# Sharing one feed-forward network between two steps, with 512 tokens side by side in its first layer

## Chip, cores and metric

The kernel runs on one core of one Trainium2 chip. The metric is device time in microseconds (us). Kernels were compared on the same chip in the same rounds; medians and ratios are of fast runs alone.

## The reference

A gated linear recurrence (batch 4, 8 heads, 768 tokens, head dimension 48) is followed by a two-layer network with a PReLU between its layers. All is fp32.

```python
for t in range(S):
    state = f[:, :, t, :, None] * state + einsum('bhd,bhe->bhde', k[:, :, t], v[:, :, t])
    y[:, :, t] = einsum('bhd,bhde->bhe', q[:, :, t], state)
# bridge: (B,H,S,D) -> (B*S, H*D) = (3072, 384)
h = x @ w_in                                        # 384 -> 2048
g = np.maximum(h, 0.0) + alpha * np.minimum(h, 0.0)
out = g @ w_out                                     # 2048 -> 384
```

## The kernel before

There are 12 steps. One step takes two batches and a chunk of 128 tokens, so T = 256 tokens. It prepares decayed keys and queries (`prepare`, VectorE and ScalarE), carries the state on (`carry`), attends (`attend`), and sends its 256 tokens through the network (`network`). The program is written as generators. A string for each step fixes the order in which their pieces are issued, and this order is kept on TensorE (PE), VectorE (DVE) and ScalarE (ACT). P is a piece of this step's preparation, Q one of the next step's, O one of carry (off and pk; then pd and the state), S one of attend (raw and qu for each half; copies into A; py; the result xT), n one of a network.

```python
def network(bp, c, x):
    xT = x["T"]
    gs = []
    for f in range(0, NF, 2):                       # NF = 16 tiles of 128, NK = 3
        ph = bank(...)                              # 128 x 512 in PSUM, 4 banks in turn
        for j in range(2):
            for kt in range(NK):
                nc.tensor.matmul(ph[:, j * T:(j + 1) * T], lhsT=w_in_sb[:, kt, ...],
                                 rhs=xT[:, kt], start=(kt == 0), stop=(kt == NK - 1))
        nc.scalar.activation(neg, phv, AF.Relu, scale=-1.0)
        for j in range(2):
            nc.vector.scalar_tensor_tensor(g[:, j], neg[:, j], om[...], phv[:, j], ALU.mult, ALU.add)
        gs.append(g)
        yield
    po = [bank(...) for u in range(U)]
    for f in range(NF):
        for u in range(U):
            nc.tensor.matmul(po[u][:, 0:DM], lhsT=gs[f // 2][:, f % 2, u * C:(u + 1) * C],
                             rhs=w_out_sb[:, f], start=(f == 0), stop=(f == NF - 1))
        if f % 4 == 3 and f != NF - 1:
            yield
    ...                                             # copies out, DMA
    yield
# cut: four strings for steps 0 to 3
usual = "O n2 S n2 S2 n O n Q n Q n S n2 S Q n S Q2 n Q"
```

A network is thus 12 pieces: 8 of the first layer and 4 of the second. While step n attends, the network of step n-1 fills PE. off, pk, pd, raw, qu and py share two pair buffers in PSUM, so each of them waits until an earlier one has been read out.

## Time and profile before

| | before |
|---|---|
| median time, 4 runs | 659.25 us (658.71 to 660.06) |
| span of the profiled execution | 658.4 us |
| PE busy | 615.5 us, 93% |
| one step from 110 us on | 50.33 us, PE busy throughout |
| one network on PE | 41.4 us |
| PE in attention, one step | 9.0 us |
| VectorE busy, one step | 33.3 us, of it 6.9 for g |

The profile's lines behind these are in the prediction. An fp32 matmul of the program is two records in the trace (1152 first-layer records for 576 products). In a row of the groups, the number after the bar is the busy time, then the mean duration of one, then the idle time ahead of it with what ended it. In a row of the timeline, that idle time stands in brackets with its releaser. The granted clock (PEclk in a page) is the share of TensorE's full clock that the profile shows as granted.

### The profile page before, as it was taken

To read this page: it belongs to the slowest core of one execution; us is meant where nothing else is said; L and a number is where in the kernel's file an instruction comes from. 1 tells how busy PE (TensorE), PEld (TensorE's weight loads), DVE (VectorE), ACT (ScalarE), POOL (GpSimd) and SP (SyncE) were. 2 spreads that over 40 slices of the span, in tenths; PEclk is the share of its full clock that TensorE was granted. 3 is DMA by queue.
4 is the path that set the end of the run, shared out by engine and by line. 5 is a ranking of instruction groups with operands and counts; after the bars stand their busy time and mean duration, and the time that the engine had idled before them with its cause. 6 is when DMAs were issued, how large, how long until landed. Compare 5 with 4: busy or idle time off the path is not lost.

```text
span 658.4 us, 17032 instructions
## 1 busy us (share of the span) xinstructions
PE 615.5 (93%) x7392; PEld 458.0 (70%) x7392; DVE 420.2 (64%) x897; ACT 267.0 (41%) x493; POOL 69.9 (11%) x109
## 2 busy tenths in 40 slices
PE   0548899999999999999999999999999999999997
PEld 0436766866876876876876876876876786786874
DVE  5999889693863685685585586486387486360220
ACT  5855882543443242451451550550460451431210
POOL 8222332000010000000000001001001000000000
PEclk9857999999999999999999999999999999999999
DMA  6979986122212122112013113023023011001000
GB/s 225 302 207 269 282 233 159 35 65 73 66 37 68 35 52 87 33 40 86 28 53 81 31 62 81 26 66 80 26 66 81 26 34 25 26 2 25 24 1 24
DMA packets 29129, 53.03 MB, mean 81 GB/s; under 512 B 4320, under 2 KB 16864, under 8 KB 29056
## 3 DMA queue, kind: packets, MB, share of 16 engines
q0 software_dynamic: 9616, 27.92, 15.4%
q1 hardware_dynamic: 13584, 21.63, 10.6%
q10 hardware_dynamic: 5856, 2.40, 1.7%
q8 instruction: 58, 0.95, 0.6%
q14 instruction: 15, 0.12, 0.1%
HBM read 36.21 MB, written 4.72 MB: 62 GB/s over the span
## 4 chain that ended last, share of the span: by engine, by line
PE 84%; issue 7%; POOL 4%; DVE 2%; ACT 1%; DMA 1%; POOLq 0%
PE po L502 36%; PE ph L486 35%; PE py L456 3%; PE qu L431 3%; PE raw L416 3%; PE pk L369 2%; PE pd L381 2%; POOL w_in_sb L191 1%; PE off L356 1%; POOL w_out_sb L191 1%; DMA w_out_sb<-w_out_lead 1%; DVE us L289 0%; POOL vs L138 0%; ACT A L340 0%; POOL vs L247 0%
## 5 line engine op out<-in xcount | busy, mean ns | idle before, releaser
L486 PE MATMUL ph<-xT,w_in_sb 128*128 128x256 f32 x1152 | 264.3, 387 | 10.3 <-DMA xT<-y 10.3
L502 PE MATMUL po<-w_out_sb,g 128*128 128x384 f32 x768 | 253.0, 488 | 0.3 <-DMA w_out_sb<-w_out_lead 0.3
L486 PEld LDWEIGHTS ph<-xT,w_in_sb 128*128 128x128 f32 x1152 | 218.1, 192 | 44.7 <-DMA w_in_sb<-w_in_lead 11.3
L502 PEld LDWEIGHTS po<-w_out_sb,g 128*128 128x128 f32 x768 | 144.9, 190 | 97.7 <-DMA w_out_sb<-w_out_lead 0.9
L494 DVE SCALAR_TENSOR_TENSOR g<-neg,om,ph 128x256 f32<-128x256 f32 x192 | 83.1, 476 | 152.0 <-ACT neg L491 151.9
L491 ACT ACTIVATE neg<-ph 128x512 f32<-128x512 f32 x96 | 57.7, 601 | 152.8 <-PE ph L486 124.8
L508 ACT COPY o<-po 128x384 f32<-128x384 f32 x24 | 11.5, 478 | 115.2 <-PE po L502 115.2
L436 DVE COPY_PREDICATED ad<-mquad,qu 128x224 f32<-128x224 int32 (+6 forms) x168 | 50.3, 300 | 8.5 <-DVE ad L422 0.5
L465 ACT COPY y<-py 128x512 f32<-128x512 f32 x24 | 12.9, 591 | 81.2 <-PE py L456 81.2
L289 DVE TENSOR_TENSOR us<-us,fs 128x768 f32<-128x768 f32 (+2 forms) x72 | 44.5, 618 | 0.3
L422 DVE COPY_PREDICATED ad<-mraw,raw 128x256 f32<-128x256 int32 (+1 forms) x96 | 42.3, 441 | 2.7
L445 ACT COPY A<-ad 32x256 f32<-32x256 f32 x96 | 38.4, 400 | 3.8 <-DVE ad L436 2.5
L391 DVE TENSOR_TENSOR vs<-vs,f 48x768 f32<-48x768 f32 x20 | 19.1, 953 | 30.4 <-PE py L456 30.0
L275 ACT COPY us<-qd 128x256 f32<-128x256 f32 x48 | 29.6, 666 | 12.2 <-DVE qd L258 7.4
L258 DVE TENSOR_TENSOR qd<-qd,f 128x768 f32<-128x768 f32 (+2 forms) x36 | 27.1, 752 | 8.2 <-ACT qd L253 8.2
L340 ACT COPY A<-q 48x512 f32<-48x512 f32 x48 | 29.6, 617 | 6.3 <-DMA xT<-y 5.5
L237 POOL DMA_DIRECT2D k<-in_kT x11 | 8.4, 761 | 222.6 <-PE raw L416 197.6
L456 PEld LDWEIGHTS py<-A,vs 128*64 128x64 f32 x768 | 25.1, 145 | 7.2 <-issue 6.2
L431 PE MATMUL qu<-us,k 48*32 48x112 f32 x1536 | 26.4, 265 | 2.6 <-DVE us L289 1.7
L456 PE MATMUL py<-A,vs 128*64 128x64 f32 x768 | 26.9, 231 | 0.9 <-DVE vs L397 0.8
L356 PE MATMUL off<-q,kh 48*32 48x32 f32 x768 | 9.4, 199 | 18.3 <-DVE q L307 18.3
L416 PEld LDWEIGHTS raw<-qd,k 48*32 48x32 f32 x1536 | 18.1, 108 | 10.6 <-issue 10.2
(64 smaller groups left out, 451.1 us busy)
## 6 DMA issues: line engine op xcount, KB each, us to landing
w_in_raw<-in_w_in SPq DMA_DIRECT2D x12, 511.8 KB, 5.9
w_out_raw<-in_w_out SPq DMA_DIRECT2D x12, 511.8 KB, 5.8
f<-in_fT POOLq DMA_DIRECT2D x11, 512.0 KB, 4.1
q<-in_qT POOLq DMA_DIRECT2D x11, 512.0 KB, 4.1
k<-in_kT POOLq DMA_DIRECT2D x11, 512.0 KB, 4.3
out<-o SPq DMA_DIRECT2D x24, 192.0 KB, 1.9
vs<-in_v POOLq DMA_DIRECT2D x22, 192.0 KB, 3.5
w_in_sb<-w_in_lead POOLq DMA_DIRECT2D x12, 256.0 KB, 6.1
```

Source lines behind the costliest of these rows:

```text
L275: nc.scalar.copy(q4[:, :, :, r], qdv[r][:, :, :, 0])
L289: nc.vector.tensor_tensor(us[:, :, UO[m]:UO[m] + 4 * n].rearrange("p g (i r) -> p g i r", r=4), us[:, :, skip:skip + 4 * n].rearrange("p g ...
L416: nc.tensor.matmul(raw[DB * j:DB * (j + 1), par, hp * C:hp * C + QW], lhsT=k[r_, g * DB:(g + 1) * DB], rhs=qd[r_, g], start=True, stop=True)
L422: nc.vector.copy_predicated(adu[:, :, :, d:4], mraw[:, d, :, d:4].bitcast(I32).unsqueeze(1).broadcast_to((128, H, NB, n)), rv[:, :, QO[d]: ...
L431: nc.tensor.matmul(qu[DB * j:DB * (j + 1), par, hp * UW + 4:(hp + 1) * UW], lhsT=k4[r_, g * DB:(g + 1) * DB], rhs=us[r_, g, 4:UW], start=T ...
L436: nc.vector.copy_predicated(ad[:, u, :, :, 4 * m:DB], mquad[:, lo:lo + n].bitcast(I32).unsqueeze(1).unsqueeze(1).broadcast_to((128, 2, HP, ...
L445: nc.scalar.copy(A[s_, u, :, s_], ad[s_, u].rearrange("p r h t -> p (r h) t"))
L456: nc.tensor.matmul(py[64 * par:64 * par + 64, u, o:o + CH], lhsT=vs[bp][:, cc, u, hd * D:hd * D + 64], rhs=A[:, u, par * HP + hp, CH * cc: ...
L486: nc.tensor.matmul(ph[:, j * T:(j + 1) * T], lhsT=w_in_sb[:, kt, (f + j) * 128:(f + j + 1) * 128], rhs=xT[:, kt], start=(kt == 0), stop=(k ...
L491: nc.scalar.activation(neg, phv, AF.Relu, scale=-1.0)
L494: nc.vector.scalar_tensor_tensor(g[:, j], neg[:, j], om[:, f + j:f + j + 1], phv[:, j], ALU.mult, ALU.add)
L502: nc.tensor.matmul(po[u][:, 0:DM], lhsT=gs[f // 2][:, f % 2, u * C:(u + 1) * C], rhs=w_out_sb[:, f], start=(f == 0), stop=(f == NF - 1))
```

## The change

The last eight steps (chunks 2 to 5 of both batch pairs) share a network in twos. The first layer then has 512 moving columns for one loaded weight tile instead of 256. The intent: half as many first-layer matmuls and weight loads, and half as many VectorE operations behind them. A pair's network can begin only when both its steps have attended, so the order strings from step 4 on are new. The core of the diff (in code and diffs, `...` stands for what is cut):

```diff
-    def network(bp, c, x):
-        xT = x["T"]
-        for f in range(0, NF, 2):
+    def network(xs):
+        n = len(xs["steps"]) * T
+        per = 512 // n
+        xT = xs["T"]
+        for f in range(0, NF, per):
             ...
-                    nc.tensor.matmul(ph[:, j * T:(j + 1) * T], ..., rhs=xT[:, kt], ...)
+                    nc.tensor.matmul(ph[:, j * n:(j + 1) * n], ..., rhs=xT[:, kt, 0:n], ...)
+            # second half of a pair's g: in the buffers where raw weights came in
-        po = [...]
+        for k, (bp, c) in enumerate(xs["steps"]):
+            po = [...]                              # as before, once for each step of the pair
...
+        "S n2 S Q S n O Q n O S n Q2 n S2 n3 Q",       # step 4:  9 network pieces
+        "P S O S O Q S Q n2 S Q2 S2 n Q2",             # step 5:  3
-    usual = "O n2 S n2 S2 n O n Q n Q n S n2 S Q n S Q2 n Q"
+    usual = (
+        "S n4 O n2 S n S Q n3 O S Q n Q2 n S n2 Q n3 S",   # steps 6, 8, 10:  17
+        "O n S n P S n Q S n Q n O Q S Q n Q S2 Q n",      # steps 7, 9, 11:   7
+    )
```

Networks that are ready queue up, and each `n` takes the next piece of the queue. What remains after the last step is issued at the end, without attention between: 24 pieces instead of 12.

More of the change, by code (lines that the diff above doesn't have):

```diff
@@ L220, in halves @@
         return slice(CH * cc, CH * cc + CH), slice(CH * (1 - cc), CH * (1 - cc) + D)
-    def fill():
-        while True:
-            b = bank("warm")
-            nc.tensor.matmul(b[:, 0:256], lhsT=ones[:, 0:128], rhs=ones[:, 0:256], start=True, stop=True)
-            yield
     def prepare(bp, c, x):
@@ L465, in attend @@
             nc.scalar.copy(y[:, u].rearrange("p h t -> p (h t)"), py[:, u])
-        xT = x["T"] = work.tile([128, NK, T], F32, tag="xT", name=f"xT_{i}")
+        xs = x["xs"]
+        if "T" not in xs:
+            xs["T"] = work.tile([128, NK, B // U * T], F32, tag="xT", name=f"xT_{i}")
+        t0 = xs["steps"].index((bp, c)) * T
+        xT = xs["T"][:, :, t0:t0 + T]
         for hd in range(H):
@@ L476, in attend @@
         yield
-    def network(bp, c, x):
-        i = f"{bp}_{c}"
-        xT = x["T"]
+    def network(xs):
+        i = "{}_{}".format(*xs["steps"][0])
+        n = len(xs["steps"]) * T
+        per = 512 // n
+        xT = xs["T"]
         gs = []
-        for f in range(0, NF, 2):
+        for f in range(0, NF, per):
             ph = bank(f"ph{f}_{i}")
-            for j in range(2):
+            for j in range(per):
                 for kt in range(NK):
-                    nc.tensor.matmul(ph[:, j * T:(j + 1) * T], lhsT=w_in_sb[:, kt, (f + j) * 128:(f + j + 1) * 128],
-                                     rhs=xT[:, kt], start=(kt == 0), stop=(kt == NK - 1))
-            neg = work.tile([128, 2, T], F32, tag="neg", name=f"neg{f}_{i}")
-            phv = ph.rearrange("p (j t) -> p j t", j=2)
-            nc.scalar.activation(neg, phv, AF.Relu, scale=-1.0)
-            g = work.tile([128, 2, T], F32, tag="g", name=f"g{f}_{i}", bufs=8)
-            for j in range(2):
-                nc.vector.scalar_tensor_tensor(g[:, j], neg[:, j], om[:, f + j:f + j + 1], phv[:, j],
-                                               ALU.mult, ALU.add)
-            gs.append(g)
-            yield
-        po = [bank(f"po{u}_{i}") for u in range(U)]
-        for f in range(NF):
-            for u in range(U):
-                nc.tensor.matmul(po[u][:, 0:DM], lhsT=gs[f // 2][:, f % 2, u * C:(u + 1) * C], rhs=w_out_sb[:, f],
-                                 start=(f == 0), stop=(f == NF - 1))
-            if f % 4 == 3 and f != NF - 1:
-                yield
-        for u in range(U):
-            o = work.tile([128, DM], F32, tag="o", name=f"o{u}_{i}")
-            nc.scalar.copy(o, po[u][:, 0:DM])
-            t0 = ((U * bp + u) * NC + c) * C
-            nc.sync.dma_start(out=out[t0:t0 + C], in_=o)
-        yield
@@ new lines, in network @@
+                    nc.tensor.matmul(ph[:, j * n:(j + 1) * n], lhsT=w_in_sb[:, kt, (f + j) * 128:(f + j + 1) * 128],
+                                     rhs=xT[:, kt, 0:n], start=(kt == 0), stop=(kt == NK - 1))
+            neg = work.tile([128, 512], F32, tag="neg", name=f"neg{f}_{i}")
+            nc.scalar.activation(neg, ph, AF.Relu, scale=-1.0)
+            if per == 2 or f < NF // 2:
+                g = work.tile([128, 512], F32, tag="g", name=f"g{f}_{i}", bufs=8)
+            elif f % 2 == 0:
+                both = work.tile([128, 2, 512], F32, tag="raw", name=f"g{f}_{i}", bufs=RAWS)
+                g = both[:, 0]
+            else:
+                g = both[:, 1]
@@ new lines, in network @@
+            for j in range(per):
+                nc.vector.scalar_tensor_tensor(g[:, j * n:(j + 1) * n], neg[:, j * n:(j + 1) * n], om[:, f + j:f + j + 1],
+                                               ph[:, j * n:(j + 1) * n], ALU.mult, ALU.add)
+                gs.append(g[:, j * n:(j + 1) * n])
+            yield
+        for k, (bp, c) in enumerate(xs["steps"]):
+            po = [bank(f"po{u}_{bp}_{c}") for u in range(U)]
+            for f in range(NF):
+                for u in range(U):
+                    t = k * T + u * C
+                    nc.tensor.matmul(po[u][:, 0:DM], lhsT=gs[f][:, t:t + C], rhs=w_out_sb[:, f],
+                                     start=(f == 0), stop=(f == NF - 1))
+                if f % 4 == 3 and f != NF - 1:
+                    yield
+            for u in range(U):
+                o = work.tile([128, DM], F32, tag="o", name=f"o{u}_{bp}_{c}")
+                nc.scalar.copy(o, po[u][:, 0:DM])
+                t0 = ((U * bp + u) * NC + c) * C
+                nc.sync.dma_start(out=out[t0:t0 + C], in_=o)
+            yield
@@ L530, in begin, with networks @@
         if n >= len(steps):
-            return [None] * 4
-        x = {}
-        return [stage(*steps[n], x) for stage in (prepare, carry, attend, network)]
-    with tc.manual_schedule(engines={mybir.EngineType.PE, mybir.EngineType.DVE, mybir.EngineType.Activation}):
-        prep, car, att, net = begin(0)
-        filling = fill()
-        before = None
-        for n in range(len(steps) + 1):
-            coming, carried, following, after = begin(n + 1)
-            on = pieces | {"P": prep, "O": car, "S": att, "z": filling, "n": before, "Q": coming}
-            for key in (first[n] if n < len(first) else usual).split():
+            return [None] * 3
+        x = {"xs": groups[n]}
+        return [stage(*steps[n], x) for stage in (prepare, carry, attend)]
+    groups = []
+    for n, (bp, c) in enumerate(steps):
+        if c < 2 or bp == 0:
+            groups.append({"steps": [(bp, c)]})
+        else:
+            groups[-1]["steps"].append((bp, c))
+            groups.append(groups[-1])
+    ready = []
+    def networks():
+        for xs in ready:
+            yield from network(xs)
+    with tc.manual_schedule(engines={mybir.EngineType.PE, mybir.EngineType.DVE, mybir.EngineType.Activation}):
+        prep, car, att = begin(0)
+        net = networks()
+        for n in range(len(steps)):
+            coming, carried, following = begin(n + 1)
+            on = pieces | {"P": prep, "O": car, "S": att, "n": net, "Q": coming}
+            for key in (first[n] if n < len(first) else usual[n % 2]).split():
                 for _ in range(int(key[1:] or 1)):
@@ L545 @@
                         next(on[key[0]])
-            before, prep, car, att, net = net, coming, carried, following, after
+            if groups[n]["steps"][-1] == steps[n]:
+                ready.append(groups[n])
+            prep, car, att = coming, carried, following
+        for _ in net:
+            pass
 def _level_masks():
```

## The prediction

> **What bounds the kernel now.** I read the page first: its busy shares, its slices and its costliest groups.
>
> ```profile
> PE 615.5 (93%) x7392; PEld 458.0 (70%) x7392; DVE 420.2 (64%) x897; ACT 267.0 (41%) x493; POOL 69.9 (11%) x109
> ...
> PE   0548899999999999999999999999999999999997
> ...
> PEclk9857999999999999999999999999999999999999
> ...
> L486 PE MATMUL ph<-xT,w_in_sb 128*128 128x256 f32 x1152 | 264.3, 387 | 10.3 <-DMA xT<-y 10.3
> L502 PE MATMUL po<-w_out_sb,g 128*128 128x384 f32 x768 | 253.0, 488 | 0.3 <-DMA w_out_sb<-w_out_lead 0.3
> L486 PEld LDWEIGHTS ph<-xT,w_in_sb 128*128 128x128 f32 x1152 | 218.1, 192 | 44.7 <-DMA w_in_sb<-w_in_lead 11.3
> L494 DVE SCALAR_TENSOR_TENSOR g<-neg,om,ph 128x256 f32<-128x256 f32 x192 | 83.1, 476 | 152.0 <-ACT neg L491 151.9
> ```
>
> TensorE is busy 93% of the span, and the slices show that what is missing lies in the first six slices (weights arriving) and in the last. A busy PE may still be pipelined slack, so I went to the chain that ended last, in order of time, for one middle step and for the end:
>
> ```profile
> 313.20 5.18 PE ph L486 x24
> ...
> 331.00 7.97 PE ph L486 x36
> 338.96 10.32 PE po L502 x32
> 349.29 2.02 PE py L456 x64
> ...
> 613.68 20.72 PE ph L486 x96
> 634.40 20.65 PE po L502 x64
> ```
>
> No other engine stands in this stretch of the chain. The last network stands alone: 20.72/96 = 215.8 ns for each first-layer record and 20.65/64 = 322.7 ns for each second-layer one. In the middle of the kernel, 32 second-layer records take 10.32 us, again 322.5 ns each. So the interleaved network streams as fast as the bare one: nothing is hidden in the "busy". One network costs 41.4 us. The windows view, one window for each step of the steady part, shows the rest:
>
> ```profile
> 210.75:261.09 50.34, 50.34 (x619) 37.48 (x618) 33.32 (x70) 17.16 (x33) 3.38 (x5) 1.00 0.20 57
> 261.09:311.42 50.33, 50.33 (x618) 37.47 (x617) 33.34 (x70) 19.42 (x37) 3.38 (x5) 1.00 0.20 56
> ```
>
> The columns are the length, then the busy time of PE, PEld, DVE, ACT and POOL. A step is 50.33 us, PE is busy for all of it, the granted clock is 1.00, DVE works 33.3 us. Attention therefore takes PE 50.3 - 41.4 = 9.0 us a step. From about 103 us to the end PE streams without a gap: **the bound is TensorE's streaming itself**, and the time can fall only by making PE do less or by mending the start.
>
> **What the Trainium skill says.** "TensorE: Matmul & The Clock Gate", section "Wait — 56ns, not 53.3ns?": start to start is N/2.4 ns plus about 2.5 ns fixed per matmul, once warm. "FP8 and Floating Point Precision", section "TensorE Precision Notes": true fp32 takes four passes. The program issues 48 first-layer products a step (16 tiles by 3) and the trace holds 96 records, so a record is two passes: 512/2.4 + 2.5 = 215.8 ns and 768/2.4 + 2.5 = 322.5 ns. The trace agrees to the tenth of a ns. The first page's "LDWEIGHTS" section gives columns/1.2, thus 107 ns for 128; here it is 190 to 192 ns. It differs, but it stays below 215.8 and is hidden. "Perfetto Trace Analysis", section "Optimizing Scalar/DVE Operations", says that each DVE operation has a fixed access overhead, more on PSUM, so larger operations pay it less often. The trace agrees in kind: in the groups with shapes kept apart, at L289 a 128x256 operation takes 423 ns and a 128x512 one 684 ns, 162 ns less than twice as long.
>
> **The change, part by part.**
>
> *Wider first layer.* Eight steps hold 8 x 96 = 768 records of 256 columns. They become 384 records of 512. Columns streamed are the same; what goes is 384 fixed costs: 384 x 2.5 ns = **-1.0 us**. A wide record should be 1024/2.4 + 2.5 = 429.2 ns (estimate from the two widths above). Weight loads are halved for these steps, but they were hidden: no gain.
>
> *ACT and DVE.* ACT evicts the same 512-wide banks at 601 ns, as many as before. DVE replaces two 256-wide operations by one of 512: 476 + (684 - 423) = 737 ns against 952. Each pair of steps has 16 such operations in place of 32; over four pairs 64 x 0.215 = 14 us of DVE duration is saved. DVE has 17 us a step to spare, so this is worth **0 us** on the path where PE is dense.
>
> *Second layer, outputs, memory.* Same 512 records of 384 columns in these steps; the second half of g borrows the buffers in which raw weights came in, free by then. **0 us**.
>
> *Where the network's work lies.* This is the part that can cost. I counted the pieces in the order strings (a first-layer piece is 2.59 us, a second-layer piece 5.16 us, twelve to a step's network). Steps 0 to 3 keep their strings, so the start, with its 43 us of idle PE, stays. Before, every later step held 12 pieces. Now step 4 has 9, step 5 has 3, then even steps have 17 and odd ones 7, and 24 pieces follow the last step. In the even steps PE has 16 x 2.57 + 5.16 + 9.0 = 55 us and DVE 26.4 (33.3 less the 6.9 of g) + 16 x 0.74 = 38; in the odd ones PE has 7 x 5.16 + 9.0 = 45 and DVE 26.4. PE stays the bound there. The bare end of 83 us is dense too: the before's end shows it.
>
> But steps 4 and 5 have one network between them, since a pair cannot start until both its halves are attended. PE work: 2 x 9.0 + 41.4 = **59.4 us**. DVE must do two steps of attention (2 x 26.4, less some 2 that may lag) and g of network 3 (6.9): **58 us**. The two are equal, so each wait that one has for the other shows. Placing them by hand, from trace durations (raw+qu 1.7 us, off and pk 1.7, pd 1.1; DVE's evictions of one raw/qu pair 4.2 us, from the timeline at 226.28 to 230.55): in step 4 the second layer's second bank waits for a late g, and off/pk for a pair buffer, about **2 us**. Step 5 opens with raw, qu, off, pk, raw, qu, pd and no network between them; with two pair buffers, pk waits for DVE's first eviction, raw for ACT, pd for DVE again: about 11 us for 6.2 us of work, **5 us** idle. At the end of step 5 the last second-layer piece runs out while DVE is still making step 6's keys and queries, which qu of step 6 needs: **2 to 3 us**. That is 9 to 10; DVE's busy time by union is a little under the elapsed times I added, so I take **+8 us**.
>
> *Hand-over of xT.* The wide first layer starts after py, one second-layer piece and raw+qu: 5.16 + 1.7 = 6.9 us. In the timeline at 301 us, py ends at 300.9, the last transfer is issued by 306.2 and lands some 2 to 2.8 us later, but the part for the first 128 rows is issued first, some 5.7 us after py. **0 to 1 us** over four hand-overs.
>
> Sum: 659.1 - 1.0 + 8 + 0 to 1 = **666 us**.
>
> **The rivals.** *Dense throughout:* the strings of steps 4 and 5 were plainly placed with care, and if PE finds work in all of them only the 1.0 us (and a few tenths from fewer switches between attention and network) remains: 657 to 658. For it: DVE and PE sums are within 2 us of each other, and DVE's g is cheaper later. Against it: no network is left for step 5 to put between its small matmuls. *Starved harder:* steps 4 and 5 become a pure latency chain over PE, DVE and ACT, ACT's xT issues block its copies (the before's waits show ACT held 5.5 us by them once), and gaps of over 3 us let the clock fall, as in the slices around 20 to 60 us where 7 and 5 tenths were granted beside idle PE. That would add 5 to 8 us more: 671 to 674. *A real gain from fewer weight loads:* if loads, 458 us of PEld, shared the path, halving 768 of them would save tens of us; the spacing of exactly 215.8 ns against a 190 ns load speaks against it. It would give 640 or less. *DVE's relief shortening the path:* only where DVE bounds, that is in step 5, where g is already over; nothing.
>
> **Range and chances.** The floor is some 657 because PE's streaming is fixed; the term that may vary is the idle in steps 4 and 5, 0 to 14 us. I choose 666, with 656 to 672 for 8 in 10. A gain of 2% needs 646, for which no idle time is there to be taken: 0.02. A loss of 2% needs over 672.3, so 13 us of idle: 0.11. Within 2%: 0.87.
>
> **What would show it.** Right: first-layer records of 512 columns spaced at 429 ns, second-layer ones at 322.5; PE gaps of 6 to 10 us in sum between about 215 and 285 us and nearly none after; DVE's g at some 740 ns; an end of 82.5 us with only ph and po. The width's step is wrong if a wide record is not 429 ns. The placement step is wrong if PE has no gaps in steps 4 and 5, or if gaps return at each start of a pair with xT as releaser. The whole is wrong if the time before 210 us moves, since nothing there changes.

## The result, and the profile after

| | before | changed |
|---|---|---|
| median of 4 runs | 659.25 us | 667.37 us (664.29 to 669.22) |
| again, in a later round | 659.66 us (11 runs) | 665.41 us (664.72 to 666.78, 4 runs) |
| ratio, first and later round | | 1.0117 (1.0077 to 1.0158), 1.0090 (1.0075 to 1.0105) |
| PE records | 7392 | 7008 |

A ratio is the mean time of one kernel's fast runs over that of the other's of the same rounds, so it is not quite the ratio of the medians quoted. The change costs about 1%.

The changed kernel's page, busy shares and slices:

```profile
PE 616.2 (93%) x7008; PEld 386.7 (58%) x7008; DVE 412.8 (62%) x833; ACT 265.3 (40%) x493; POOL 68.2 (10%) x109
...
PE   0648899999999988999999999999999999999997
...
PEclk9987999999999997999999999999999999999999
```

71 us of weight loading and 7 us of VectorE time are gone by union (overlapping stretches counted once), and PE is as busy as it was. New are the two eights among the nines of PE (the 15th and 16th slice, 232 to 265 us), with a lower granted clock in the second of them: this is where step 5 opens. The groups with shapes kept apart, and the end of the timeline of PE:

```profile
L487 PE MATMUL ph<-xT,w_in_sb 128*128 128x512 f32 x384 | 168.8, 595 | 0.0
...
L501 DVE SCALAR_TENSOR_TENSOR g<-neg,om,ph 128x512 f32<-128x512 f32 x64 | 47.0, 745 | 74.1 <-ACT neg L491 73.5
```

```profile
576.41 41.36 PE L487 MATMUL ph<-xT,w_in_sb 128*128 128x512 f32 x96
617.61 41.44 PE L511 MATMUL po<-w_out_sb,g 128*128 128x384 f32 x128
```

In the bare end (the last network, with no attention beside it) 96 wide records start at 576.41 and the next kind at 617.61: 429.2 ns each, as worked out. The last pair's network is as dense as a single one. Step 5 in the same timeline, start and duration first:

```profile
248.42 1.08 PE L349 MATMUL off<-q,kh 48*32 48x32 f32 x64 [2.07 <-DVE ad L415]
250.82 1.94 PE L362 MATMUL pk<-ident,ks 128*128 128x128 f32 x8 [1.31 <-DVE ad L429]
252.69 1.34 PE L409 MATMUL raw<-qd,k 48*32 48x80 f32 x64
253.92 1.59 PE L424 MATMUL qu<-us,k 48*32 48x112 f32 x64
256.12 1.15 PE L374 MATMUL pd<-vs,ksn 64*64 64x48 f32 x64 [0.61 <-PE qu L424]
257.20 10.59 PE L511 MATMUL po<-w_out_sb,g 128*128 128x384 f32 x32
```

From the first raw of step 5 (244.60 us) to the second layer at 257.20 go 12.6 us, for which 6.2 us of matmul work was counted. 4.0 us are waits of PE (2.07, 1.31 and 0.61) for VectorE's evictions. VectorE began to read out the first raw only at 246.42 us, after preparation, though the last matmul of raw was over at 245.51. The profile puts the wait of pd down to qu, but qu was over at 255.51; pd takes the buffer of the second raw, which VectorE had read out at 256.02, 0.10 us before pd began:

```profile
246.42 1.86 DVE L415 COPY_PREDICATED ad<-mraw,raw 128x256 f32<-128x256 int32 x4
...
254.12 1.90 DVE L415 COPY_PREDICATED ad<-mraw,raw 128x256 f32<-128x256 int32 x4 [3.44 <-PE raw L409]
```

Of the remaining 2.4 us, 2.1 are the same small matmuls running slower: off, pk, raw and qu last 1.08, 1.94, 1.34 and 1.59 us here, against 0.76, 1.09, 0.92 and 1.07 us for the same blocks in step 6. The windows view gives the reason; its columns end with granted clock, DMA share and GB/s:

```profile
246.00:248.00 2.00, 0.35 (x26) 0.11 (x11) 1.84 (x7) 1.97 (x4) 0.00 (x0) 1.00 0.00 0
248.00:250.00 2.00, 1.08 (x64) 0.97 (x64) 1.76 (x6) 0.62 (x3) 0.00 (x0) 0.60 0.03 8
250.00:252.00 2.00, 1.18 (x6) 1.21 (x7) 0.60 (x3) 0.82 (x3) 0.00 (x0) 0.50 0.00 0
252.00:254.00 2.00, 2.00 (x76) 1.49 (x82) 0.00 (x0) 1.18 (x3) 0.00 (x0) 0.50 0.00 0
254.00:256.00 2.00, 1.51 (x67) 1.26 (x64) 1.78 (x4) 1.97 (x3) 0.73 (x1) 0.70 0.28 43
```

After the first wait of 2 us the clock falls to half. Before step 4 nothing differs in kind: step 4 begins at 209.00 us here and at 210.34 us in the later profile, against 210.75 us before. From there to the end the sums are 447.65 us before (658.4 - 210.75), 453.5 us in this profile, 454.7 us in the later one: 5.9 and 7.0 us more. The parts add up to within 0.4 us: 6.4 (in the later profile 6.8) us lost at the opening of step 5, 0.7 us at pk in step 4, 0.9 us in the later profile on second-layer records still at half clock, less 1.0 us of fixed costs.

### The profile page after: what moved, and what is told of

Same layout as the page of the kernel before. It is cut to its first block, busy times and chain, and to the rows that moved or that the text cites. A ratio compares the mean times of both kernels' runs of the same rounds, so it can differ in the third digit from the quotient of the medians.

```text
span 662.5 us, 16194 instructions
## 1 busy us (share of the span) xinstructions
PE 616.2 (93%) x7008; PEld 386.7 (58%) x7008; DVE 412.8 (62%) x833; ACT 265.3 (40%) x493; POOL 68.2 (10%) x109
## 4 chain that ended last, share of the span: by engine, by line
PE 87%; DVE 8%; issue 2%; DMA 1%; POOL 1%; ACT 1%; ACTq 0%; DVEq 0%; POOLq 0%
PE po L511 37%; PE ph L487 36%; PE py L449 3%; PE qu L424 3%; PE raw L409 2%; PE pk L362 2%; PE pd L374 2%; DVE ad L429 2%; DVE us L282 1%; PE off L349 1%; DVE ad L415 1%; DMA xT<-y 1%; DVE w_in_lead L176 1%; DVE g L501 1%; DMA lvl<-in_masks 0%
## 5 line engine op out<-in xcount | busy, mean ns | idle before, releaser
L487 PE MATMUL ph<-xT,w_in_sb 128*128 128x256 f32 (+1 forms) x768 | 259.5, 494 | 11.1 <-DMA xT<-y 11.1
L487 PEld LDWEIGHTS ph<-xT,w_in_sb 128*128 128x128 f32 x768 | 145.1, 193 | 110.0 <-issue 84.0
L501 DVE SCALAR_TENSOR_TENSOR g<-neg,om,ph 128x256 f32<-128x256 f32 (+1 forms) x128 | 74.5, 610 | 96.8 <-ACT neg L491 96.0
L388 DVE TENSOR_TENSOR vs<-vs,pd 48x384 f32<-48x384 f32 x40 | 22.1, 552 | 19.2 <-PE pd L374 17.8
L268 ACT COPY us<-qd 128x256 f32<-128x256 f32 x48 | 27.3, 667 | 10.0 <-DVE qd L251 5.5
L424 PE MATMUL qu<-us,k 48*32 48x112 f32 x1536 | 27.9, 275 | 1.4 <-DVE ad L429 1.3
```

Of the source, the lines that this page charges most:

```text
L424: nc.tensor.matmul(qu[DB * j:DB * (j + 1), par, hp * UW + 4:(hp + 1) * UW], lhsT=k4[r_, g * DB:(g + 1) * DB], rhs=us[r_, g, 4:UW], start=T ...
L487: nc.tensor.matmul(ph[:, j * n:(j + 1) * n], lhsT=w_in_sb[:, kt, (f + j) * 128:(f + j + 1) * 128], rhs=xT[:, kt, 0:n], start=(kt == 0), st ...
L501: nc.vector.scalar_tensor_tensor(g[:, j * n:(j + 1) * n], neg[:, j * n:(j + 1) * n], om[:, f + j:f + j + 1], ph[:, j * n:(j + 1) * n], ALU ...
```

## The experiments

The theories were these. **A**: the whole loss is the starving of PE in step 5, where no network is left to put between attention's small matmuls, and the clock's fall that follows. **B**: pairing costs in itself (hand-over of xT, borrowed buffers, the longer end). **C**: weight loads share the path, so the halving has a large gain hidden under the loss. **D**, formed later: 48 pieces can't feed steps 1 to 5 in any order.

### Width alone undone

```diff
-                for kt in range(NK):
-                    nc.tensor.matmul(ph[:, j * n:(j + 1) * n], ..., rhs=xT[:, kt, 0:n], ...)
+                for h in range(n // T):
+                    for kt in range(NK):
+                        nc.tensor.matmul(ph[:, j * n + h * T:j * n + (h + 1) * T], ...,
+                                         rhs=xT[:, kt, h * T:(h + 1) * T], ...)
```

> The changed kernel with each 512-wide first-layer product issued as two of 256 columns again; order, pairs, buffers, ACT and DVE work as changed. Theory A: 384 more records with 2.5 ns fixed each, so 1.0 us slower than the changed kernel (about 668 against 667 us; in the bare end 192 records in 41.4 us, 215.8 ns each, for 96 at 429.2). Rival C (weight loads share the path, so that halving them was worth much): at least 5 us slower than the changed kernel.

Measured: 666.75 us median of 5, ratio 1.0100 (1.0086 to 1.0114) to the before of its rounds. The unaltered changed kernel had 1.0090 (1.0075 to 1.0105) in other rounds: 0.7 us apart, and the intervals overlap, so the times alone do not resolve 1 us. The trace does, in the bare end of this kernel:

```profile
580.47 41.60 PE L488 MATMUL ph<-xT,w_in_sb 128*128 128x256 f32 x192
621.91 41.44 PE L513 MATMUL po<-w_out_sb,g 128*128 128x384 f32 x128
```

41.44 us from one start to the next, 215.8 ns a record, against 41.20 us for the wide form: 0.24 us for one pair, 1.0 us for four. Theory C asked for 5 us and is out.

### Pairing and width undone, starved order kept

```diff
-        if c < 2 or bp == 0:
+        if True:                       # every step a group of its own
...
-    usual = ("S n4 O n2 S n S Q n3 ...", "O n S n P S n ...")
+    usual = ("O n2 S n2 S2 n O n Q n Q n S n2 S Q n S Q2 n Q",) * 2
```

> Pairing and width undone (every network by itself, 256-wide as before, and the before's order string from step 6 on), but the 9 and 3 pieces of steps 4 and 5 kept, so that two networks are left for the bare end. Theory A: the loss is in the order alone, so the time is the before plus the gaps of steps 4 and 5: 664 to 668 us, with gaps of 4 to 7 us and a half-clock stretch in step 5. Theory B (pairing itself costs): as the before, 658 to 660 us.

Measured: 667.07 us median of 5, ratio 1.0111 (1.0096 to 1.0125). No network is shared here and no matmul is wide, and the loss is there in full. The timeline of step 5:

```profile
250.29 0.75 PE L349 MATMUL off<-q,kh 48*32 48x32 f32 x64 [2.40 <-DVE ad L415]
252.68 1.94 PE L362 MATMUL pk<-ident,ks 128*128 128x128 f32 x8 [1.65 <-DVE ad L429]
```

The same two waits, with the same releasers. So the order alone makes the loss; B is not needed for it.

### Idle-filling matmuls in the waits of step 5

```diff
+    def warm(n):
+        b = bank("warm")
+        for _ in range(n):
+            nc.tensor.matmul(b[:, 0:256], lhsT=ones[:, 0:128], rhs=ones[:, 0:256], start=True, stop=True)
...
+        if (bp, c) == (1, 2): warm(4)      # ahead of off
+        if (bp, c) == (1, 2): warm(3)      # ahead of pk
```

> The changed kernel with 4 and 3 idle-filling matmuls (431 ns each) put into the two longest waits of step 5, before off and before pk; they make nothing that is used. If part of the loss is the clock that falls when PE idles (the trace after shows 0.5 to 0.7 granted from 248 to 256 us), the clock stays at 1.00, the small matmuls after the wait run at full rate and 1.5 to 3 us are won: about 664.5 us; the waits themselves stay, as busy time. If the clock costs nothing that the waits did not cost already: no change, 667 us.

Measured: 664.32 us median of 6, ratio 1.0068 (1.0053 to 1.0083): some 1.5 us less than the changed kernel's 1.0090 of other rounds, at the lower edge of what was expected; the two intervals overlap a little, so the times alone don't show it. The trace does:

```profile
246.87 1.99 PE L225 MATMUL warm<-ones 128*128 128x256 f32 x8
249.19 0.75 PE L356 MATMUL off<-q,kh 48*32 48x32 f32 x64 [0.33 <-DVE ad L424]
249.87 1.56 PE L225 MATMUL warm<-ones 128*128 128x256 f32 x6
251.60 1.07 PE L371 MATMUL pk<-ident,ks 128*128 128x128 f32 x8 [0.17 <-DVE ad L438]
252.60 0.92 PE L418 MATMUL raw<-qd,k 48*32 48x80 f32 x64
```

pk takes 1.07 us and raw 0.92 us again, and the granted clock is 1.00 in every 2 us window from 244 to 262 us. The waits stay, as busy time. From the first raw to the second layer go 11.9 us (245.18 to 257.06), against 12.6 and, in the later profile below, 13.0. So the clock's fall is a part of the loss of its own, apart from the waits.

### VectorE's relief undone

```diff
             for j in range(per):
-                nc.vector.scalar_tensor_tensor(g[:, j * n:(j + 1) * n], ...)
+                for h in range(j * n, (j + 1) * n, T):
+                    nc.vector.scalar_tensor_tensor(g[:, h:h + T], ...)
```

> The changed kernel with each 512-wide g operation on VectorE cut into two of 256 again: some 64 operations more, at 475 ns in place of half of a 740 ns one, 13 us more VectorE time in the steps after step 5. The relief of VectorE was predicted to be worth 0 us: no change against the changed kernel, within 1 us (some 667 us). Rival: the changed kernel already has a part of the win from VectorE hidden in it, and this run is 3 us or more slower.

Measured: 665.14 us median of 6; the unaltered changed kernel in the same rounds 665.41 us, ratios 1.0089 (1.0069 to 1.0109) and 1.0090 (1.0075 to 1.0105). VectorE is busy for 171.75 us between 300 and 570 us instead of 162.85 us, and the time is not longer for it. The relief is worth nothing that these runs can show.

### The changed kernel again

> The changed kernel unaltered, to have its time in the same rounds as its variants, and a second profile: the first one (662.5 us span) was its fastest run, others were 2 to 5 us longer. If the spread comes from where the clock's fall meets step 5, this profile shows a longer half-clock stretch there with the same idle gaps; if from the start, steps 0 to 2 end later.

Measured: 665.41 us median of 4, and a profile of 665.0 us against 662.5 us. Windows of this profile:

```profile
250.00:252.00 2.00, 0.34 (x10) 0.30 (x3) 1.41 (x6) 1.26 (x4) 0.00 (x0) 0.65 0.03 8
...
258.00:260.00 2.00, 2.00 (x41) 1.60 (x35) 1.83 (x6) 1.69 (x4) 0.53 (x1) 0.50 0.70 203
260.00:262.00 2.00, 2.00 (x6) 1.07 (x6) 1.88 (x5) 0.00 (x0) 0.00 (x0) 0.79 0.62 248
```

Worked out from the windows' means, half clock lasts here from about 250.6 to 260.8 us instead of 248.4 to 255.2, and it reaches into the second layer: 32 records of it take 11.45 us from start to start for 10.52. The idle waits ahead are of the same size (1.62, 1.66 and 0.44 us). The length of a wait alone doesn't decide whether the clock falls: in step 1 the same wait for pk was followed by full clock in the first profile and by half clock in this one, where another wait, of 0.54 us, had come shortly before:

```profile
69.50 1.06 PE L362 MATMUL pk<-ident,ks 128*128 128x128 f32 x8 [1.65 <-DVE ad L429]
```

```profile
69.95 1.94 PE L362 MATMUL pk<-ident,ks 128*128 128x128 f32 x8 [1.66 <-DVE ad L429]
```

Of the 2.5 us between the two profiles, 1.3 lie in the start (210.34 against 209.00 us) and 1.2 after it. The slowest run of all, 669.22 us, has no profile; what made it slow stays open.

### Spreading the network over steps 2 to 5

If A is right, taking a few pieces from steps 2 and 3 and giving them to step 5 must bring the time to the before's less 1.0 us. Pieces in steps 2, 3, 4, 5: 10, 9, 9, 8 in place of 12, 12, 9, 3. Only the four strings differ from the changed kernel. It took five tries.

```diff
+        "n2 O n S n2 S Q S n S O n Q n Q2 n P S n S Q2",
+        "n S n S Q n2 O n S2 Q n O Q2 n Q S2 Q n2",
+        "S n2 S Q S n2 O Q n O S n Q2 n S2 n2 Q",
+        "P S n2 S Q S n2 O Q n O S Q2 n S2 n2 Q2",
```

> The changed kernel with only the order strings of steps 2 to 5 altered, so that these steps hold 10, 9, 9 and 8 network pieces in place of 12, 12, 9 and 3. Theory A (the loss is the starving of TensorE in step 5, where no network is left to put between attention's small matmuls): the PE gaps and the half-clock stretch of step 5 vanish, second step of pairing and all later ones unchanged, and the time is the before less the 1.0 us of fixed costs: 656.5 to 658.5 us, about 0.2% under the before. Theory B (pairing itself costs: the hand-over of xT, the borrowed g buffers, wide banks held longer, a longer bare end): the time stays at 664 to 669 us.

Measured: 674.34 us median of 4, ratio 1.0223: slower, a miss for both numbers. Step 5's old waits were gone and three new ones had come. One of them, in PE's timeline, and one that precedes it, in VectorE's:

```profile
244.13 1.58 PE L424 MATMUL qu<-us,k 48*32 48x112 f32 x64 [4.30 <-DVE us L282]
```

```profile
226.28 1.12 DVE L388 TENSOR_TENSOR vs<-vs,pd 48x384 f32<-48x384 f32 x2 [9.18 <-PE pd L374]
```

VectorE stood 9.2 us behind a state update whose pd came late. The next step's preparation, queued behind that update, was then late for qu. Steps had become shorter: with 9 pieces a step is some 40 us (estimated from 41.4 us a network and 9.0 us of attention), so VectorE, with 33 us of work in a fixed order, has some 7 us to spare, less than this one wait. The second try moved preparation ahead:

```diff
+        "S n2 Q S n2 Q2 O n Q O S2 n Q S2 n3 Q",
+        "S n2 Q S n2 Q2 O Q n Q O S2 n S2 n3",
+        "P S n2 Q S n2 Q2 O Q n Q O S2 n S2 n2 Q",
```

> The spread order again (10, 9, 9 and 8 pieces in steps 2 to 5), mended where it failed: there raw/qu of steps 4 and 5 and one py waited 3.0 to 4.3 us for VectorE, which had sat idle before it for 4.5 to 9.2 us behind an attention block that came late, with the preparation of the next step queued behind that block. Now the preparation pieces stand ahead of the late block. Theory A (starving in step 5 is the whole loss, and the spread failed only by the order on VectorE): PE gaps after 110 us under 1 us in sum, granted clock 1.00 there, 656.5 to 659 us. Theory B (pairing costs in itself): 664 us or more, with gaps or longer matmuls after step 6. Theory D (five steps with 48 pieces can't feed PE in any order): gaps of 4 us or more remain in steps 3 to 5, 663 us or more.

Measured: a wrong result (relative error 0.32) and 687.29 us. The edit put a piece that rewrites qd ahead of a raw that still reads it. This says nothing on the theories. The third try:

```diff
+        "n S n S Q n2 O n O S2 Q n2 S2 Q n2 Q3",
+        "n2 S n S Q n Q O S2 Q n O n Q S2 n3 Q",
+        "P n S n S n O n O S2 Q n2 Q2 S2 n2 Q3",
```

> The spread of 10, 9, 9 and 8 pieces once more. The run before was wrong and slow by my own mistake: it had the first preparation piece, which rewrites qd, ahead of the second half's raw, so raw read the next step's data and waited 15.1 us for it. Now that piece stands after both halves in every step, steps 3 to 5 open with a network piece or two so that VectorE can end its queue, and moved(0) stands ahead of the next preparation where py would wait for it. Theory A (starving and the clock's fall are the whole loss): gaps after 110 us under 1.5 us in sum, no half-clock stretch, 656.5 to 659.5 us. Theory D (48 pieces can't feed five steps in any order): gaps of 4 us or more, 663 us or more. Theory B (pairing costs in itself): few gaps, and still 663 us or more.

Measured: correct, 666.28 us median of 4, ratio 1.0104. Waits of 0.98, 2.71 and 1.51 us were left in steps 4 and 5. By its number it sided with D. Its narrow twin went with it:

> The same order with 256-wide first-layer products. The fixed cost of 2.5 ns for each of 384 more records: 1.0 us slower than the third spread, and so at or just above the time of the kernel before. If weight loads mattered once TensorE is dense, 5 us or more slower.

Measured: 667.64 us median of 4, ratio 1.0125 (1.0108 to 1.0142) against 1.0104 (1.0087 to 1.0121): 1.4 us, consistent with 1.0, the intervals overlapping. The fourth try:

```diff
+        "n S n S Q n2 O n O S2 Q n2 S2 Q n2 Q2",
+        "n2 P S n S Q n Q O S2 Q n O n Q S2 n3 Q",
+        "S P n2 S n2 O Q n O S2 n Q2 S2 n2 Q3",
```

> The third spread was right but not dense: 5.2 us of gaps were left, 4.2 of them in step 5, and half clock after them. VectorE, late by some 2 us there, had stood idle another 2.3 us (234.3 to 236.7 us) before a g whose relu waited on ScalarE behind four copies of A, while raw of step 5 was ready for it. Now step 5 opens with raw/qu and two network pieces follow it, and the copies of A come after the first relu in step 4. Theory A (starving and the clock's fall are the whole loss): gaps after 110 us under 1 us in sum, clock 1.00 from 110 us on, and 656.5 to 659 us, at or under the before. Theory B (pairing costs in itself): few gaps and still 663 us or more. Theory D (48 pieces can't feed five steps in any order): new gaps of 3 us or more elsewhere.

Measured: 662.71 us median of 8, ratio 1.0049 (1.0032 to 1.0065). One wait was left, in PE's timeline:

```profile
232.47 1.08 PE L424 MATMUL qu<-us,k 48*32 48x112 f32 x64 [1.94 <-DVE us L282]
233.47 7.13 PE L487 MATMUL ph<-xT,w_in_sb 128*128 128x256 f32 x24
240.54 0.92 PE L409 MATMUL raw<-qd,k 48*32 48x80 f32 x64
```

The 24 records after it take 7.07 us from start to start for 5.2: a gap of 1.94 us cost as much again in clock. The windows, which end with granted clock, DMA share and GB/s:

```profile
234.00:236.00 2.00, 2.00 (x6) 0.50 0.00 0
236.00:238.00 2.00, 2.00 (x8) 0.67 0.00 0
```

The fifth try altered step 4's string alone:

```diff
-        "n2 P S n S Q n Q O S2 Q n O n Q S2 n3 Q",
+        "n2 P S n S Q n Q O S2 Q2 n O n2 Q S2 n2",
```

> The fourth spread left one gap after 110 us, 1.94 us before qu of step 5, which waited for the last preparation piece on VectorE, and half clock after it (24 first-layer records in 7.07 us for 5.2): 3.8 us in all, which is what separates it from the dense sum. Now step 4 has its two last preparation pieces ahead of py, and py one piece later. Theory A: no gap over 0.5 us after 110 us, no half clock, and the time is the before less 1.0 us of fixed costs and some tenths: 657.5 to 659 us. Theory B (pairing costs in itself): 661 us or more without gaps. Theory D: another gap of 2 us or more turns up.

Measured: 658.75 us median of 14 (657.10 to 660.42), the before 659.38 us median of 19; ratio 0.9995 (0.9985 to 1.0004). After 110 us no idle time of PE is left in the timeline, and the windows of this kernel and of the before from 110 us to the end read:

```profile
110.00:656.40 546.40, 543.00 (x5933) 330.98 (x5931) 316.60 (x626) 194.09 (x373) 27.86 (x41) 1.00 0.17 47
```

```profile
110.00:658.40 548.40, 545.04 (x6321) 405.02 (x6319) 324.39 (x692) 195.68 (x375) 27.77 (x41) 1.00 0.17 47
```

Measured from the first first-layer record of step 2, a point that both programs reach in the same way (108.98 and 109.97 us), it is 547.4 us against 548.4: 1.0 us less, the whole of what the width was worked out to be worth. Pairs, borrowed buffers and the long end are all in it. So B and D are out and A stands, but for the 0.7 us at pk, which lay in step 4. As a time, this version is the same as the before, not shown faster: the interval holds 1.

## Why the prediction was right

**Width, -1.0 us: right.** Wide records are 429.2 ns apart, and the dense version is 1.0 us shorter from step 2 on.

**VectorE's relief, 0: right**, and shown by undoing it. The wide g takes 745 ns, against 737 worked out.

**Placement of the network's work, +8 us: right in its mechanism and, within 2 us, in size; the terms were not.** For the opening of step 5 the prediction had 5 us; 6.4 and 6.8 us were measured. Some 4 us are waits, and nearly all the rest is the half clock, which it had only in its rival "Starved harder". It had named the waits of pk and pd for VectorE; the longest, that of off (2.07 us), it had not, and raw's wait for ScalarE did not come. For step 4 it had 2 us; 0.7 us was measured, at pk, and no wait for a second-layer bank. For the end of step 5 it had 2 to 3 us; there was none, since VectorE finished us at 275.69 us and qu began at 275.75. So a missing clock term and an end wait that did not come nearly cancelled, which is luck. One of the prediction's own signs failed: the gaps of PE between 215 and 285 us sum to 4.7 and, in the later profile, 4.4 us, not 6 to 10. The sum of 8 stands for 5.9 and 7.0 us after step 4 plus the 1.0 that the width gives back.

**Hand-over of xT, 0 to 1 us: right.** No wait for xT shows at a pair's start; the first 24 wide records of step 6 take 10.63 us where later ones take 10.49 from start to start.

**Nothing changes before 210 us: right in kind**, with step 4 reached 0.4 to 1.8 us earlier; executions of the before differ by 1.4 us among themselves in the same rounds and by up to 2.6 us in later ones.

The rival "dense throughout" was no description of the changed kernel, but it is what the fifth spread reached: the before's time less 1.0 us, by trace. "A real gain from fewer weight loads" fell: 71 us of loading went without effect.

## What to carry to other kernels

Where TensorE streamed without a gap here, the number of matmuls mattered only through their fixed cost, 2.5 ns a record; multiply the records saved by that cost before building anything. Merging two pieces of filler work delays the first of them, so ask which stretch will have nothing to fill with, and compare the sums of the engines there. A schedule that is dense at one step length need not stay so at a shorter one: shifting a few pieces turned idle time of VectorE, whose order is fixed, into TensorE's waits, and a wait of 1.94 us cost as much again because the clock fell after it.

## What the Trainium skill lacked or had wrong

- "TensorE: Matmul & The Clock Gate", section "Why this matters for your kernels", advises no idle gaps over about 3 us between bursts. The page also tells of a clock that oscillates when TensorE idles briefly but often between groups of matmuls, without a length. Here one wait of 1.94 us, between two blocks of small matmuls, was followed by half clock: 7.07 us for 24 records instead of 5.2. Waits of 0.98 us and 0.71 us were not. Between these no length divides them: of the two waits of 1.65 and 1.66 us shown above one was and one was not, and in the before one of 2.18 us (up to 80.20 us) was not. Fillers put where the changed kernel waited 2.07 and 1.31 us held the clock at 1.00.
- The same page's "LDWEIGHTS" section gives columns/1.2, 107 ns for 128 columns. The network's fp32 loads of 128 columns take 190 to 192 ns here in the mean; pk's transposes, of 128 columns too, load in 140 ns (median).
- No page says how an fp32 matmul appears in a trace. Here it is two records, each as long as two passes, and the fixed 2.5 ns falls once on a record: 215.8 ns at 256 columns, 322.5 at 384, 429.2 at 512.
